# A DFT along time split by output index modulo 6, with score masks moved between engines and a new written order

## The chip, the core and the metric

The kernel runs on one core of a Trainium2 chip. The core has five engines that run side by side, each with its own queue in order: TensorE (PE in the profile, with weight loads as PEld) multiplies matrices into PSUM, VectorE (DVE), ScalarE (ACT) and GpSimd (POOL) do elementwise work, and SyncE (SP) here only starts DMA transfers. GpSimd does not read PSUM in this kernel; VectorE and ScalarE do. The metric is the device time of one execution in microseconds (us); lower is better.

## The reference: what is computed

Inputs are q, k, v of shape (4 batches, 8 heads, 768 steps, 64) and two weight matrices, 512 x 2048 and 2048 x 512. All are float32, and so is the output (4, 768, 512).

```
state = gamma[h] * state + outer(k[t], v[t]);  y[t] = (q[t] @ state) / 8      # for each batch and head, 768 steps
x     = y with the heads side by side: (4, 768, 512)
u     = x + real(fft over the 512 columns of (fft over the 768 steps of x))
un    = (u - mean(u)) / sqrt(var(u) + 1e-6)                                    # over the 512 columns
out   = u + relu(un @ w_ch1) @ w_ch2
```

gamma is 1 - 2^(-5-h) for head h, one constant a head.

## The kernel before

**Retention.** Steps are cut into 6 chunks of 128, heads into 4 pairs. Within a chunk the scores K Q^T are formed on TensorE, masked (causal, with a power of gamma folded in) and multiplied with V; between chunks a 64 x 64 state per head is carried. For batches 1 to 3 and pair i the units are: `lq`, `lk`, `lv` (or `l`) start the loads (L242); `cq`, `ck`, `cv` cast to float16 on GpSimd (L461 or L466, L477, L486); `t` or `tq`, `tk` transpose q and k, on TensorE with ScalarE copies (L655, L660, L665) or by DMA (L651, L673, L678); `s` builds the chunk states (L708, then L713 and L715); `a` makes and masks the scores of two chunks (`a_unit`: matmuls L689, one VectorE multiply with a table, L691; three units a pair); `y` forms the output of a head (L729, L732) and ScalarE writes it into x (L739).

**Mixing.** The DFT along time uses symmetries. `fs` (L758) adds and subtracts the two halves of the time axis, which separates even and odd output frequencies; `fd` (L785) and `fe` (L799, L801) do the like for the columns, giving `ee`: four groups (cosine or sine, two column blocks), each with a part for even and one for odd frequencies, each three blocks of 128 steps. A unit `f` (`s1_unit`) multiplies one group with a cosine or sine table (`csp`, `ssp`, 193 frequencies for each parity): two parities x three blocks, six matmuls of 193 columns (L861), and one copy that interleaves the parities into `g` (L864). `gr` makes a reversed copy (L868). `x` (`s2_unit`, L1015 to L1025) does the DFT along the columns and writes the rows of u, `X` adds x on GpSimd (L1048, L1050). `n` takes mean and variance on VectorE, `u` centres the row and rounds it to float16 on ScalarE (L1064), `r` is the root on ScalarE and the reciprocal on VectorE (L1074, L1076). Batch 0 has a layout of its own and is not touched.

**MLP.** `U` transposes the centred rows (by TensorE, L1087, or by DMA, L1083). Batch 0 runs as `i`, `h` and `c` with `O` (L1118, L1105, L1140, L1130). Batches 1 to 3 run as `H` (first matrix, L1193, with a relu, L1098 on ScalarE or L1095 on VectorE) and, for the second matrix, a scheme with seven products instead of eight: `w` and `j` form sums (L1181, L1211), `p` multiplies (L1242), `q` adds the product into the rows (L1256) and starts the output.

**Order.** Up to about 36 us a list FIRST is worked off (batch 0's retention and mixing, building of the tables). Then a written list LATER names every unit in the order in which it is issued. Each instruction is tied to the one before it on its own engine, so every engine's queue follows the list, and an instruction that waits holds back all that stand behind it on its engine. A name is the unit, its indices (batch, pair or row block, part) and, after @, the engine that evicts: a is ScalarE, v VectorE, s two halves on ScalarE, b one half on each, d a transpose by DMA. PSUM has five buffers for mixed use (`ps_g`) and, in this part, three for the MLP (`ps_pm`). SyncE's queue follows the list too: loads, DMA transposes and outputs.

Of the kernel before, what the change touches and what calls it, by code (L numbers as in the profile page):

```python
# [11 lines left out]
AF = mybir.ActivationFunctionType  # L12
ALU = mybir.AluOpType
f32 = mybir.dt.float32
# [5 lines left out]
P = 128  # L20
# [7 lines left out]
KN = 2 * NK  # L28
XW = 260
# [23 lines left out]
i02 U01@v Z x04 x03 i12 U02@a x05 i13 X04 i10 cq10 c0000 c0001 X05 TB l10 i20 l11 X03 l12 i22  # L53
cq11 l13 c0002 i11 i03 i21 n05 u05 ck10 n04 lq20 cv10 c0010 t10 w10 n03 u03 r00 c0003 i23 c0011
c0012 a101 s100 pz11 U03@a ck11 t11 c0020 a102 s101 a100 c0021 cv11 a110 s110 s111 ck12 u04 a112
cq12 c0013 y100 a111 cq13 c0022 cv12 U05@a ck13 cv13 y101 t12 U04@v c0023 O00 y110 O01 pz00 s120
h018@a s121 h012@a s130 y111 t13 h01C@v pz01 s131 lk20 a120 lv20 lq21 h017@a a122 pz10 h01A@a
h011@a a121 h013@v O02 h01D@a a131 a132 y121 y120 a130 h01B@a cq20 tq20 h015@a fs10 y131 y130
h01E@v h010@a h016@a fs11 fd10 g10 h014@a fd11 w20 fe11 c0100 ck20 tk20 h019@a lk21 lv21 lq22
lk22 fe10 w31 c0101 a201 c0102 r01 cv20 f110@a a202 f111@a f100@a f101@a g112 cq21 gr12@a a200  # L60
s200 cq22 h01F@a x11 tq21 X11 gr10@a c0110 x10 gr11@a lv22 s201 c0120 n11 X10 gr13@a n10 lq23
lk23 ck21 tk21 w11 c0121 c0122 w40 x12 u11 lv23 X12 cq23 u10 c0103 O03 c0111 c0112 cv21 U11@a
ck22 U10@v x14 n12 c0113 O04 c0123 y200 x13 H102@a a212 r10 x15 s210 X13 cv23 n13 y201 tq22
H107@a O05 H100@a a211 w21 a210 H106@a ck23 s211 u13 tk23 U13@d w30 H103@a H101@s j10104 w41
j10204 j10304 cv22 H105@a s230 u12 H104@s j10148 y210 tk22 y211 tq23 p101 q101 j10248 p102
j10404 q102 lq30 lk30 j10448 p104 p106 q106 lv30 lq31 j10348 U12@v p105 cq30 s231 p107 q105 s220
a221 a220 H112@a p103 q103 a231 a230 a232 X14 a222 s221 H110@a X15 n15 q107 ck30 H114@a n14
H115@s y231 lk31 y230 fs21 lv31 y220 lq32 y221 H113@s H116@s H111@s H117@s fs20 fd21 g20 u14
fd20 j11104 fe20 u15 j11148 U14@d r11 j11204 fe21 p111 q111 p112 cv30 j11404 j11248 p114 f200@a
p115 q115 f201@a tq30 j11448 gr21@a j11304 cq32 f210@a gr22@a U15@d f211@a p116 q116 gr23@a  # L70
j11348 g212 p113 cq31 lk32 gr20@a lv32 q112 q113 x20 X20 x21 p117 H124@a q117 tq31 x23 H120@s
H121@v H122@s ck31 X21 n21 x25 H123@a u21 n20 j12104 j12204 j12404 cv31 H125@a lq33 j12304
H127@a r12 tk31 H126@s j12148 x22 p121 p122 u20 q121 p124 p125 U21@d r20 j12248 p126 U20@d q122
q125 j12448 q126 X22 j12348 s300 s301 X23 tk30 p123 q123 n23 cq33 lk33 a312 p127 s310 H200@a
a301 u23 ck32 lv33 n22 H204@s q127 tk32 a300 H206@s a302 H203@a a311 u22 X25 x24 cv32 n25 H201@s
H202@a j20104 y300 a310 U23@d H205@s s311 U22@d H207@s j20148 y301 ck33 j20304 j20204 p201 q201
j20348 j20248 j20404 p204 p205 y310 X24 y311 q205 tq32 tk33 p206 q206 cv33 s330 p202 q202 s320
j20448 tq33 p207 n24 q207 H217@s u25 p203 a320 s321 q203 a331 u24 U24@d s331 H214@b a332 a330
# [20 lines left out]
def kernel(  # L99
# [241 lines left out]
    def qt_zeros():  # L341
        for j in range(2):
            nc.vector.memset(qts[j][0:D, 1], 0.0)
            nc.vector.memset(qts[j][D:P, 0], 0.0)

    m2 = const.tile([P, 1], f32, tag="m2c")
    odd = const.tile([P, 1], f32, tag="oddc")

# [1084 lines left out]
```

## Time and profile before

| | |
|---|---|
| three runs | 238.18, 238.02, 237.14 us, median 238.02 |
| profiled execution | 237.16 us, of which span 235.2 us |
| PE busy | 221.0 us, 94% of the span |
| DVE busy | 203.7 us, 87% |
| ACT busy | 137.5 us, 58% |
| POOL busy | 82.5 us, 35% |
| HBM | 27.26 MB read, 6.29 MB written |

How to read it: the span runs from the first to the last instruction of the profiled execution. Busy time of PE counts matmuls that overlap each other once; the length shown for a single matmul includes its way through the array, so the pace of a row of matmuls is read from the start of one group to the start of the next. In a row of the groups stand line, engine, operation, what is written and read with shapes and count, then busy us and mean ns of one, then the idle time ahead of them and what ended it. In a row of the timeline stand start, length, engine, line, operation and count, and in brackets the idle time before. TensorE has no idle time over 1.1 us after the first 36 us.

### The profile page before, as it was taken

The page shows a single profiled execution, that of the slowest core. Times are in us where ns is not written, and L with a number is a line of the kernel's source. Part 1 is how long each engine was busy: PE and PEld are TensorE (multiplying, and loading weights), DVE is VectorE, ACT ScalarE, POOL GpSimd, SP SyncE. Part 2 cuts the span into 40 slices and gives each one's busy share as a digit, 9 for nine tenths or more (in the row PEclk, how much of TensorE's full clock was granted, in tenths as well). Part 3 has the DMA queues.
Part 4 walks back from the last instruction along what each step waited for, and adds up shares of the span by engine and source line. Part 5 has one row for each costly group of instructions (what it writes and reads, how often), then busy time and mean ns, then how long its engine had stood idle before and what let it go on. Part 6 is the DMA issues. An engine that isn't in the chain of part 4 may idle for free.

```text
span 235.2 us, 6193 instructions
## 1 busy us (share of the span) xinstructions
PE 221.0 (94%) x2407; PEld 181.9 (77%) x2407; DVE 203.7 (87%) x505; ACT 137.5 (58%) x322; POOL 82.5 (35%) x148
## 2 busy tenths in 40 slices
PE   0888999998999999999999999999999999999993
PEld 0366778855776756999999999998999888898882
DVE  8799986887899999999999899989997996749673
ACT  5989758368777565751867735736529736062230
POOL 8378902654613076702604565500002330020000
PEclk9999999999999999999999999999999999999999
DMA  7999999999999999979699995894002140502202
GB/s 173 236 267 246 237 207 207 217 240 251 202 230 185 215 190 226 223 153 211 167 213 189 204 170 146 174 154 133 4 4 89 30 108 0 104 33 47 89 0 92
DMA packets 100956, 36.83 MB, mean 157 GB/s; under 512 B 91456, under 2 KB 97984, under 8 KB 100928
## 3 DMA queue, kind: packets, MB, share of 16 engines
q1 hardware_dynamic: 96704, 32.25, 68.3%
q0 software_dynamic: 4224, 4.19, 10.8%
q8 instruction: 19, 0.31, 0.6%
q14 instruction: 9, 0.07, 0.1%
HBM read 27.26 MB, written 6.29 MB: 143 GB/s over the span
## 4 chain that ended last, share of the span: by engine, by line
PE 65%; DMA 17%; DVE 4%; POOL 4%; SPq 3%; ACT 3%; issue 2%; POOLq 0%; ACTq 0%; DVEq 0%
PE psh L1193 27%; PE ps L1242 21%; DMA q<-in_q_dram 6%; DMA v<-in_v_dram 5%; PE psc L1140 3%; DMA wide<-in_k_dram 2%; PE wkA L689 2%; DMA k<-in_k_dram 2%; PE pq L1015 2%; PE ps L861 2%; DMA unT<-un 2%; PE ps L842 2%; SPq L242 1%; PE wkY L732 1%; PE pq L927 1%
## 5 line engine op out<-in xcount | busy, mean ns | idle before, releaser
L1098 ACT ACTIVATE ht<-psh 128x256 f16<-128x256 f32 (+2 forms) x112 | 49.3, 467 | 45.6 <-PE psh L1193 37.9
L1193 PE MATMUL psh<-unT,w 128*128 128x256 f16 x576 | 68.0, 273 | 0.2 <-DMA unT<-un 0.2
L1193 PEld LDWEIGHTS <-w 128*128 128x128 f16 x576 | 55.4, 98 | 6.8 <-DMA unT<-un 0.5
L1242 PEld LDWEIGHTS <-ht 128*128 128x128 f16 x440 | 41.3, 98 | 5.1 <-ACT ht L1098 0.5
L1048 POOL TENSOR_TENSOR u<-u,x 128x256 f32<-128x256 f32 x21 | 13.6, 646 | 68.4 <-DVE u L1022 57.3
L1242 PE MATMUL ps<-wide,ht 128*128 128x256 f16 x216 | 27.8, 273 | 0.0
L1211 DVE TENSOR_TENSOR ht<-ht 128x512 f16<-128x512 f16 (+2 forms) x57 | 22.4, 411 | 3.6 <-ACT ht L1098 3.4
L1140 PE MATMUL psc<-w,ht 128*128 128x512 f16 x96 | 23.5, 379 | 1.0 <-DVE ht L1095 1.0
L691 DVE TENSOR_TENSOR atm<-wkA,maskp 128x512 f16<-128x512 f32 x36 | 23.3, 677 | 0.0
L466 POOL TENSOR_SCALAR q16z<-q 128x384 f16<-128x384 f32 x16 | 8.4, 545 | 34.6 <-DMA q<-in_q_dram 23.3
L1095 DVE TENSOR_SCALAR ht<-psh 128x256 f16<-128x256 f32 (+2 forms) x25 | 13.5, 540 | 7.0 <-ACT ht L1098 5.5
L1242 PE MATMUL ps<-w,ht 128*128 128x256 f16 x144 | 18.3, 273 | 0.0
L715 DVE SCALAR_TENSOR_TENSOR s<-s,gk,wkK 128x128 f16<-128x128 f16 x48 | 16.3, 342 | 1.8 <-ACT s L713 0.5
L1064 ACT ACTIVATE un<-u,stats 128x512 f16<-128x512 f32 x21 | 14.7, 722 | 4.6 <-DVE stats L1060 4.6
L739 ACT ACTIVATE x<-wkY,gexp 128x384 f16<-128x384 f32 x24 | 13.1, 593 | 6.5 <-PE wkY L732 6.5
L477 POOL TENSOR_SCALAR kd<-k,gexp 128x384 f16<-128x384 f32 x22 | 12.7, 589 | 12.0 <-DMA k<-in_k_dram 11.0
L1256 DVE SCALAR_TENSOR_TENSOR u<-ps,stats,u 128x256 f32<-128x256 f32 (+2 forms) x27 | 15.2, 563 | 1.3 <-PE ps L1242 1.1
L1256 DVE SCALAR_TENSOR_TENSOR ob<-ps,stats,u 128x256 f32<-128x256 f32 (+2 forms) x27 | 14.8, 558 | 1.4 <-PE ps L1242 1.2
L1140 PEld LDWEIGHTS <-ht 128*128 128x128 f16 x96 | 9.0, 98 | 8.8 <-issue 1.1
L1059 DVE BATCH_NORM_STATS2 bst<-u 128x6 f32<-128x512 f32 x21 | 14.3, 681 | 0.7 <-POOL u L1050 0.7
L1050 POOL TENSOR_TENSOR u<-u,x 128x256 f32<-128x256 f32 x21 | 13.4, 636 | 0.0
L689 PE MATMUL wkA<-qTz,kT 128*128 128x256 f16 x72 | 12.5, 272 | 0.2 <-DVE atm L691 0.2
(203 smaller groups left out, 424.2 us busy)
## 6 DMA issues: line engine op xcount, KB each, us to landing
out_dram<-ob SPq DMA_DIRECT2D x23, 256.0 KB, 2.3
k<-in_k_dram SPq DMA_DIRECT2D x14, 384.0 KB, 5.4
v<-in_v_dram SPq DMA_DIRECT2D x14, 384.0 KB, 5.9
q<-in_q_dram SPq DMA_DIRECT2D x12, 384.0 KB, 6.5
w<-in_moe_w_ch_dram POOLq DMA_DIRECT2D x8, 512.0 KB, 10.8
wide<-in_q_dram SPq DMA_DIRECT2D x4, 384.0 KB, 5.9
wide<-in_v_dram SPq DMA_DIRECT2D x2, 384.0 KB, 6.0
wide<-in_k_dram SPq DMA_DIRECT2D x2, 384.0 KB, 5.7
```

The source lines that it names most:

```text
L689: nc.tensor.matmul(wk[:, c2], st["kT"][:, c, :], st["qT"][:, :, c, :], start=True, stop=True)
L691: nc.vector.tensor_tensor(out=st["atm"][:, 2 * part:2 * part + 2], in0=wk, in1=maskp[:, PAIR_ORDER[i]].unsqueeze(1).to_broadcast([P, 2, 2, ...
L715: nc.vector.scalar_tensor_tensor(out=s16[:, c], in0=s16[:, c - 1], scalar=gk2[:, hp:hp + 1], in1=wk[:, c - c0], op0=ALU.mult, op1=ALU.add)
L1048: nc.gpsimd.tensor_tensor(out=u[:, kb, 0:256], in0=u[:, kb, 0:256], in1=x[:, kb, 0, 1:257], op=ALU.add)
L1059: nc.vector.bn_stats(bst, u[:, kb, :])
L1064: nc.scalar.activation(un, u[:, kb, :], AF.Identity, bias=stats[:, kb, 0:1], scale=-1.0)
L1098: nc.scalar.activation(dst, src, AF.Relu, bias=0.0, scale=-1.0)
L1140: nc.tensor.matmul(psc_of[b, rb], ht16[:, fb, rb3 * P:(rb3 + 1) * P], w216[:, fb, :], start=(fb == 0), stop=(fb == NFB - 1))
L1193: nc.tensor.matmul(psh[:, t], w116[:, cb, fb * P:(fb + 1) * P], unT[:, cb, g * 256:(g + 1) * 256], start=(cb == 0), stop=(cb == 3))
L1211: nc.vector.tensor_tensor(out=out_, in0=x, in1=y, op=op)
L1242: nc.tensor.matmul(dst, lhsT, rhs[:, c0:c1], start=(n == 0 and (name is not None or k == 5 and m == 1)), stop=(n == 7), skip_group_check=True)
L1256: nc.vector.scalar_tensor_tensor(out=out_, in0=in_, scalar=r, in1=u_, op0=ALU.mult, op1=ALU.add)
```

## The change

Five things change together.

1. Units `z1`, `z2`, `z3` (`six_fold`) are new: five VectorE operations for each of batches 1 to 3 combine the three blocks of `ee` by sums and differences, into a new tile `zz` and in place. `s1_unit` then makes the output frequencies in six classes modulo 6, 64 or 65 columns each: four matmuls of 128 columns and two of 64 and 65 in place of six of 193. Its copy reads the six classes from PSUM at a stride of -64 and writes `g` in order. `zz` uses the buffer of `eo`.
2. Units `V00` to `V11` (`six_unit`) are new: ScalarE copies rearrange the tables `csp` and `ssp` in place, once, after batch 0 is done with them.
3. `a_unit` can mask by ScalarE and GpSimd: two ScalarE copies with a constant scale, one for each head, then a GpSimd `affine_select` in place that puts zeros below the diagonal. 25 of the 36 score units take it, 11 stay on VectorE.
4. `K0` (`root_unit`) runs a square root early on ScalarE, so that its table is loaded there. `u` may run on GpSimd (three of 21 do), and `x` gets a variant on ScalarE and GpSimd that the list does not use.
5. The list LATER is new. It holds the same units and the nine new ones. Some evictions go to another engine, and nearly all units move: the zero fills (`Z`) and the half tables (`TB`) come later, casts, loads, scores and folds of batches 1 to 3 mostly earlier.

```diff
+    def six_unit(e, part):
+        tab = tabs[e]
+        def run():
+            for par in range(2):
+                src = tab[:, par, 2 - 2 * part, 0:192].rearrange("p (m i) -> p i m", i=3)[:, ::-1]
+                if part == 0:
+                    src = src[:, 0:3:2] if par else src[:, 0:2]
+                n = 3 if part else 2
+                nc.scalar.copy(tab[:, par, 1 + part, 0:64 * n].rearrange(
+                    "p (s m) -> p s m", s=n), src)
+            if part:
+                nc.scalar.copy(tab[:, 0, 2, 192:193], tab[:, 0, 0, 192:193])
...
-    def a_unit(b, i, part):
+    def a_unit(b, i, part, eng):
...
+            dst = st["atm"][:, 2 * part:2 * part + 2]
+            if eng == "v":
+                nc.vector.tensor_tensor(
+                    out=dst, in0=wk,
+                    in1=maskp[:, PAIR_ORDER[i]].unsqueeze(1).to_broadcast([P, 2, 2, P]),
+                    op=ALU.mult)
+                return
+            for h2 in range(2):
+                nc.scalar.activation(dst[:, :, h2], wk[:, :, h2], AF.Copy, bias=0.0,
+                                     scale=float(gam[2 * PAIR_ORDER[i] + h2] ** (-P)))
+            nc.gpsimd.affine_select(out=dst, in_=dst, compare_op=ALU.is_ge, fill=0.0, base=0,
+                                    pattern=[[0, 2], [0, 2], [1, P]], channel_multiplier=-1)
...
+    def six_fold(b):
+        def run():
+            z = fd[b]["zz"] = fp.tile([P, 4, 6, P], f16, tag="eo", name="zz")
+            ee = fd[b]["ee"]
+            x0, x1, x2 = (ee[:, :, :, n] for n in range(3))
+            nc.vector.tensor_tensor(out=z[:, :, 0:2], in0=x1, in1=x2, op=ALU.add)
+            nc.vector.tensor_tensor(out=z[:, :, 2:4], in0=x2, in1=x1, op=ALU.subtract)
+            for par, op in ((0, ALU.subtract), (1, ALU.add)):
+                nc.vector.tensor_tensor(out=x1[:, :, par], in0=x0[:, :, par], in1=x1[:, :, par],
+                                        op=op)
+            nc.vector.tensor_tensor(out=x2, in0=x0, in1=z[:, :, 0:4:3], op=ALU.add)
...
     def s1_unit(b, e, cb, eng):
         def run():
-            tab = csp if e == 0 else ssp
-            ps = ps_g.tile([P, 2, NK], f32, tag="g", name="ps1", padded_shape=[P, 2, 256])
-            for par in range(2):
-                for sb in range(3):
-                    nc.tensor.matmul(ps[:, par, :], fd[b]["ee"][:, 2 * e + cb, par, sb, :],
-                                     tab[:, par, sb, :], start=(sb == 0), stop=(sb == 2))
-            dst = fd[b]["g"][:, 2 * e + cb].rearrange("p (i t) -> p t i", t=2)
-            (nc.vector.tensor_copy if eng == "v" else nc.scalar.copy)(dst, ps)
+            ps = ps_g.tile([P, KG], f32, tag="g", name="ps1", padded_shape=[P, 512])
+            t = ps[:, 0:384].rearrange("p (s m) -> p s m", s=6)
+            n = 2 * e + cb
+            ee, z, tab = fd[b]["ee"][:, n], fd[b]["zz"][:, n], tabs[e]
+            od, ev = (tab[:, par, 2, 0:192].rearrange("p (s m) -> p s m", s=3) for par in (1, 0))
+            for dst, x, w, y, v in (
+                    (t[:, 0:5:4], ee[:, 1, 1], od[:, 0:3:2], z[:, 1], tab[:, 1, 1, 0:128]),
+                    (t[:, 1:4:2], ee[:, 0, 1], ev[:, 0:2], z[:, 2], tab[:, 0, 1, 0:128])):
+                nc.tensor.matmul(dst, x, w, start=True, stop=False, skip_group_check=True)
+                nc.tensor.matmul(dst, y, v.rearrange("p (s m) -> p s m", s=2), start=False,
+                                 stop=True, skip_group_check=True)
+            nc.tensor.matmul(t[:, 2], ee[:, 1, 2], od[:, 1], start=True, stop=True,
+                             skip_group_check=True)
+            nc.tensor.matmul(ps[:, 320:385], ee[:, 0, 2], tab[:, 0, 2, 128:193], start=True,
+                             stop=True, skip_group_check=True)
+            src = bass.AP(tensor=ps.tensor, offset=ps[:, 320:321].offset,
+                          ap=[list(ps.ap[0]), [1, 65], [-64, 6]])
+            dst = fd[b]["g"][:, n].rearrange("p (m r) -> p m r", r=6)
+            (nc.vector.tensor_copy if eng == "v" else nc.scalar.copy)(dst, src)
...
+    def root_unit():
+        nc.scalar.activation(last[:, 4:5], epsT, AF.Sqrt, bias=0.0, scale=1.0)
```

Stretches of the new list that the prediction speaks of; the first is the start, then the first masks of batch 1 with `r00`, the load ahead of `a131`, the first new fold, and the last one:

```
i02 U01@v x04 X04 x03 i10 U02@a x05 i13 X05 i12 K0 cq10 Z c0000 c0001 i22 i20 i03 i11 ...
... t10 c0020 s100 c0021 cv11 s101 t11 r00 a100@a c0010 a102@v a101@v l13 cq12 s110 ck12 c0011 u05@a a111@v u03@a c0022 a110@a y100 ...
... y101 t12 lq20 s111 TB ... s130 h01C@a h012@a s131 a132@v cq20 a131@a y121 h015@a lv20 lq21 lk21 a130@v y120 ...
... y131 y130 lv21 cv21 O02 cv20 h017@a h010@a h014@a h01F@a h01E@a h011@a h013@a h019@a ck21 V11 fs10 h01D@a fs11 h01A@a fd10 fd11 g10 fe10 fe11 z1 h01B@v c0100 pz10 V01 a201@v c0110 f110@a f100@a ...
... fe31 u24@a U24@d p212 p216 p214 p215 q212 q216 p217 z3 j21404 j21448 g312 H220@a f301@v ...
```

In the list before, `r00` stands behind `t10 w10 n03 u03` and ahead of `c0003 i23 c0011 c0012`, and no root comes earlier; the `f` units follow `fe` of the same half.

More of the change, by code (lines that the diff above doesn't have):

```diff
@@ L59 @@
[L59 to L64, printed above, removed]
```

129 lines of the change are left out of this document (74 added, 55 removed).

## The prediction

> **What bounds the kernel now.** I read the page's engine sums first, then a table by stage, and TensorE's order of work at the places that the change touches. The page and the stage table (columns: length, busy us and instructions of PE, PEld, DVE, ACT, POOL, then TensorE clock, DMA share, GB/s):
>
> ```profile
> span 235.2 us, 6193 instructions
> PE 221.0 (94%) x2407; PEld 181.9 (77%) x2407; DVE 203.7 (87%) x505; ACT 137.5 (58%) x322; POOL 82.5 (35%) x148
> ...
> 50.00:80.00 30.00, 28.98 (x296) 19.67 (x295) 26.11 (x60) 22.00 (x41) 11.75 (x19) 1.00 1.14 222
> 80.00:120.00 40.00, 39.82 (x431) 32.67 (x429) 38.77 (x94) 24.60 (x64) 17.97 (x30) 1.00 1.09 200
> 120.00:170.00 50.00, 50.00 (x549) 45.40 (x548) 47.54 (x119) 29.33 (x75) 16.84 (x27) 1.00 0.77 151
> 170.00:200.00 30.00, 30.00 (x306) 27.09 (x304) 26.19 (x68) 16.91 (x42) 6.06 (x10) 1.00 0.17 45
> 200.00:231.00 31.00, 30.71 (x296) 26.97 (x294) 22.18 (x58) 9.38 (x26) 1.23 (x2) 1.00 0.23 56
> ```
>
> From 50 us on TensorE works 28.98 of 30, 39.82 of 40, then 50 of 50, 30 of 30 and 30.71 of 31 us, at full clock. So it sets the time, and a shorter stream of matmuls shortens the kernel, as long as it stays fed in its written order. VectorE is close behind (47.54 of 50), ScalarE is half idle. TensorE's idle time in these rows is 1.02 + 0.18 + 0.29 = 1.5 us, and 1.0 of that is one wait, shown below. The other views are TensorE's order of work (start, length, what, idle before and what ended it) and the groups of instructions of each engine (busy sum, mean ns, idle before).
>
> **The split by six (gain).** One unit of the old time-axis DFT is six matmuls of 193 columns; 12 such units run (batches 1 to 3). Their pitch is read from the starts of successive rows, not from the modelled lengths:
>
> ```profile
> 76.74 0.81 PE L1105 MATMUL psh<-unT,w 128*128 128x384 f16 x4
> 77.39 1.03 PE L1140 MATMUL psc<-w,ht 128*128 128x512 f16 x4
> 78.26 0.38 PE L689 MATMUL wkA<-qTz,kT 128*128 128x256 f16 x2
> 78.47 1.03 PE L1140 MATMUL psc<-w,ht 128*128 128x512 f16 x4
> 79.34 0.68 PE L861 MATMUL ps<-ssp,ee 128*128 128x193 f16 x6
> 79.85 0.38 PE L689 MATMUL wkA<-qTz,kT 128*128 128x256 f16 x2
> ...
> 72.64 0.31 PE L729 MATMUL wkY<-s,qTz 128*128 128x64 f16 x5
> 72.78 0.34 PE L732 MATMUL wkY<-v,atm 128*128 128x64 f16 x6
> 72.96 0.31 PE L729 MATMUL wkY<-s,qTz 128*128 128x64 f16 x5
> ...
> 128.38 0.40 PE L1015 MATMUL pq<-gk,g16r 128*128 128x129 f16 x4
> 128.61 0.27 PE L1193 MATMUL psh<-unT,w 128*128 128x256 f16 x1
> ```
>
> Six of 193 columns take 79.85 - 79.34 = 0.51 us. Four of about 128 take 128.61 - 128.38 = 0.23, eleven of 64 take 72.96 - 72.64 = 0.32, or 0.029 each. The new unit has four of 128 and two of 64 or 65: 0.23 + 0.06 = 0.29 us. Gain 12 x (0.51 - 0.29) = 2.6 us, all on the bounding engine. The page "TensorE: Matmul & The Clock Gate" of the Trainium skill, section "Back-to-back issue gap", speaks against this: it gives about 81 ns a matmul at 128 columns when each has its own weight load. By it the new unit would take 6 x 0.081 = 0.49 us and the gain would be 0.3 us. The rows above do not agree: with a weight load before each matmul, they show 57 ns at 128 columns and 29 ns at 64.
>
> **The fold for it (cost on VectorE).** `six_fold` adds five tensor_tensor in float16 for each batch: three on 1024 elements, two on 512. The same kind:
>
> ```profile
> L1181 DVE TENSOR_TENSOR wide<-w 128x1024 f16<-128x1024 f16 x2 | 1.4, 689 | 0.0
> L1211 DVE TENSOR_TENSOR ht<-ht 128x512 f16<-128x512 f16 x48 | 19.6, 427 | 2.1 <-ACT ht L1098 1.9
> L785 DVE TENSOR_TENSOR eo<-xab 128x768 f16<-128x768 f16 x12 | 6.1, 551 | 0.0
> L799 DVE TENSOR_TENSOR ee<-eo 128x768 f16<-128x768 f16 x6 | 3.4, 560 | 0.0
> L758 DVE TENSOR_TENSOR xab<-x 128x768 f16<-128x768 f16 x6 | 3.3, 589 | 0.0
> ```
>
> 3 x 0.69 + 2 x 0.43 = 2.9 us a batch, and the first `f` matmul waits for it. In batch 1 the new list puts 11 `h` units (0.65 us each: 77.39 - 76.74), two `c` parts (0.87 each: 79.34 - 78.47) and a score unit (0.21) between the last `y` and `f110`: 9.1 us of TensorE. VectorE's chain there is four `fs` (2.4), four `fd` (2.2), four `fe` (2.2), the mean row (0.5) and `z1` (2.9), 10.2 by means; queued instructions overlap by some 8% (L785: 12 x 551 ns in 6.1 us), and half of the `fs` can start before the last `y`. So TensorE waits 0 to 1.5 us; I take 0.6. In batch 2, 3.5 us of matmuls lie between `z2` and `f211`, in batch 3 under 1.1 but VectorE reaches `z3` early, behind two adds: 0 to 1, I take 0.3. `six_unit` rearranges the tables with nine ScalarE copies and one single-column one, about 2.5 us once, priced by the nearest rows; they are part of the ScalarE sum below. The eviction reads PSUM at a stride, 390 values for 386: the same 0.60 us, bounds 0 and +0.1 on ScalarE.
>
> ```profile
> L868 ACT COPY g16r<-g 128x384 f16<-128x384 f16 x11 | 5.4, 515 | 0.1
> L1017 ACT COPY qn<-pq 128x128 f32<-128x128 f32 x18 | 5.0, 279 | 5.2 <-PE pq L1015 4.8 <-DVE u L1025 0.3
> L864 ACT CAST g<-ps 128x386 f16<-128x386 f32 x12 | 6.7, 600 | 3.8 <-PE ps L861 3.6
> ```
>
> **The masks (VectorE to ScalarE and GpSimd).** 25 of 36 score masks leave VectorE: 5 in batch 1, 10 each in batches 2 and 3. Rows:
>
> ```profile
> L691 DVE TENSOR_TENSOR atm<-wkA,maskp 128x512 f16<-128x512 f32 x36 | 23.3, 677 | 0.0
> L1098 ACT ACTIVATE ht<-psh 128x256 f16<-128x256 f32 x62 | 21.1, 385 | 25.5 <-PE psh L1193 23.9 <-issue 1.5
> L299 POOL TENSOR_SCALAR_AFFINE_SELECT maskf<-maskf 128x128 f32<-128x128 f32 x1 | 0.3, 293 | 0.0
> L284 POOL MEMSET ht<- 128x512 f16 x1 | 0.5, 515 | 0.0
> masks.py:197 POOL MEMSET ident<- 128x128 f16 x1 | 0.2, 195 | 0.0
> ```
>
> VectorE loses 25 x 0.68 = 17 us and gets 8.7 back from the folds. ScalarE gets 25 x 2 x 0.385 = 19 us. A 512-element select is not in the trace: at the memsets' slope it is 293 + (515 - 195) = 0.61 us, at four times the 128 row 1.17; I take 0.61, since the 128 row holds a start-up too. GpSimd gets 15 us (up to 29) of which it has idle plenty. The mask's path grows from 0.68 to 0.77 + 0.61 and a hand-over, some 1.5 us. In the new list the last score unit of a pair stands 1.2 to 5.7 us of matmuls ahead of its first `y`, adding the pitches of the units between (before: 1.5 to 10.3), and in the tight pairs that last one is a VectorE mask. A select is queued behind casts that wait for loads, though (idle before, and what ended it):
>
> ```profile
> 63.84 0.99 POOL L466 TENSOR_SCALAR q16z<-q 128x384 f16<-128x384 f32 x2 [1.12 <-DMA q<-in_q_dram]
> 69.58 1.15 POOL L477 TENSOR_SCALAR kd<-k,gexp 128x384 f16<-128x384 f32 x2 [4.74 <-DMA k<-in_k_dram]
> 137.68 0.82 DVE L1211 TENSOR_TENSOR ht<-ht 128x512 f16<-128x512 f16 x1
> 139.56 1.50 POOL L466 TENSOR_SCALAR q16z<-q 128x384 f16<-128x384 f32 x2
> ```
>
> In the new list `cq20` stands right ahead of the select of `a131`, and its load is issued behind the key transposes of pair 2. I price that at 0 to 2 us, taking 0.4. The last two rows show a second cost: a VectorE add of two SBUF tensors at 0.82 for 0.43 while GpSimd adds, and a GpSimd cast pair at 1.50 for 0.99 while VectorE adds. The page "SBUF — State Buffer" of the Trainium skill, section "Who interferes with whom", has the rule: the two engines share one pair of ports, as a lock. The trace agrees. With 28 more GpSimd operations it happens more often; if a third of them hit, 9 x 0.4 = 4 us on VectorE, which has 8 more to spare.
>
> **Does ScalarE become the bound?** In 50 to 80 us it has 22.0 us. Five masks add 3.9, the tables 2.5, two relus taken from VectorE 1.0, and the table load leaves (1.3): 28.1 of 30. In 80 to 120 it has 24.6 + 7.7 = 32 of 40, in 120 to 170 29.3 + 7.7 = 37 of 50. Only the first is tight, and there two or three copies of transposes a pair go through ScalarE in order:
>
> ```profile
> L660 ACT COPY qTz<-tq 64x768 f16<-64x768 f16 x8 | 6.3, 789 | 0.1
> ```
>
> **The square-root table.** The 1.0 us wait of TensorE is this chain:
>
> ```profile
> 52.81 1.28 ACT L1074 ACT_TABLE_LOAD   x1
> 54.44 0.18 DVE L1076 RECIPROCAL stats<-stats 128x3 f32<-128x3 f32 x1 [2.05 <-ACT stats L1074]
> 54.53 0.66 DVE L1095 TENSOR_SCALAR ht<-psh 128x512 f16<-128x512 f32 x1
> 55.24 1.02 PE L1140 MATMUL psc<-w,ht 128*128 128x512 f16 x4 [1.02 <-DVE ht L1095]
> ```
>
> VectorE's reciprocal waits 2.05 us for the load and the root, and the relu that TensorE wants is queued behind it. In the new list the load is ahead of `c0000`, under 1.7 us of `c` matmuls that need no new relu, and the last relu stands ahead of `r00`. I take the whole 1.0 as gain; late next is the first masked `y`, behind the ScalarE copies of two pairs' transposes: 0 to 0.7, I take 0.2. The other edits (three casts to GpSimd, some relus between engines, the three zero fills later) sit on engines with idle time: nothing, bounds -0.3 and +0.5.
>
> **Sum** for the profiled execution of 237.16 us (span 235.2): -2.6 - 1.0 + 0.6 + 0.3 + 0.4 + 0.2 = -2.1, so 235.1. The three times shown run from 237.14 to 238.18 with median 238.02, so the profiled one is a low one; the median of the new kernel I put in between, 235.3.
>
> **Rivals.** Half a percent, 1.2 us, is about what a measurement of this kernel can tell from no change.
> A: ScalarE decides between 50 and 80 us. For: 28.1 of 30, and in-order copies of transposes (0.8 each) ahead of relus. Against: VectorE ran 38.77 of 40 in the next stage with TensorE at 39.82. Price: two late chains of two transposes' copies (0.8 to 1.5 us each) give back 1.6 to 3 us, time 236.9 to 238.3.
> B, the other side: selects come late on GpSimd. Place: pairs of batches 1 to 3 where a cast or residual add is ahead of a select. Decides when the select costs 1.17 us, or a load lands over 2 us after the mask's ScalarE half. Each late pair stops TensorE by 0.6 to 1.5 us; six of twelve pairs late is 3.6 to 9 us on top of the 235.3: 239 to 244. For: the 4.74 us wait above. Against: from 120 us on GpSimd was idle two thirds of the time.
> C: the split saves nothing, since a matmul's weight load bounds it: the unit stays at 0.5 us, time 235.3 + 2.3 to 2.6, 237.6 to 237.9. Against: the rows at 64 columns. The page on TensorE named above is its only support.
>
> **How the numbers follow.** Forecast (faster) 0.60, A 0.17, C 0.03, B 0.20. The likeliest one's own range is 233.3 to 236.8: the lower end takes every new wait as zero and the other edits at their -0.3 (237.16 - 3.9). The whole range reaches into B, to 240.0, leaving out half of B and a little below. Faster 0.60, same 0.20, slower 0.20.
>
> **What would show it.** Right: the new `ps1` matmuls at a pitch of 0.29 us a unit, the 1.0 us wait gone, TensorE's busy sum down by 2 to 3, masks' ScalarE halves at 0.39, selects near 0.6. Wrong: TensorE waiting on `atm` from GpSimd (B), on ScalarE copies or relus between 50 and 80 us (A), on `ee` or `zz` for more than 1.5 us, or 0.08 us a matmul (C).

## The result and the profile after

Twenty executions of each kernel gave a median of 237.03 us for the changed kernel (235.89 to 237.84) and 238.19 us for the kernel before (236.97 to 240.03). The ratio is 0.9955, 95% interval 0.9936 to 0.9975: 0.45% faster, and the medians differ by 1.2 us, where 2.9 (238.19 less 235.3) were forecast. The gain is clear of zero, but under the half percent that the prediction counted as no change. The profiled execution of the changed kernel took 237.41 us, 0.4 above its median, while the one before took 237.16, 1.0 below its median. So the two traces differ by +0.25 us where the medians differ by -1.2, and single waits have to be compared over several traces.

The page of the changed kernel (span, then busy us, share and instructions of each engine, then two of its costliest groups), and below it the stage table with the columns of the table before:

```profile
span 235.7 us, 6275 instructions
PE 220.4 (94%) x2407; PEld 179.0 (76%) x2407; DVE 197.5 (84%) x491; ACT 150.5 (64%) x383; POOL 102.6 (44%) x176
...
L724 POOL TENSOR_SCALAR_AFFINE_SELECT atm<-atm 128x512 f16<-128x512 f16 x25 | 15.9, 650 | 18.7 <-issue 11.7
L722 ACT ACTIVATE atm<-wkA 128x256 f16<-128x256 f32 x50 | 15.8, 395 | 5.3 <-PE wkA L712 5.1
```

```profile
50.00:80.00 30.00, 29.13 (x296) 19.40 (x296) 25.58 (x66) 25.81 (x63) 13.98 (x22) 1.00 1.08 227
80.00:120.00 40.00, 39.25 (x417) 31.22 (x415) 37.51 (x93) 29.00 (x84) 27.89 (x43) 1.00 1.18 218
120.00:170.00 50.00, 49.43 (x556) 44.30 (x555) 46.39 (x116) 34.06 (x94) 24.15 (x38) 1.00 0.70 133
170.00:200.00 30.00, 29.58 (x300) 26.39 (x300) 25.65 (x63) 15.96 (x44) 8.35 (x13) 1.00 0.21 49
...
```

The work did move as described: VectorE lost 6 us, ScalarE gained 13, GpSimd 20. But TensorE, which was without idle time from 120 to 200 us before, now shows 0.57 and 0.42 us of it there, and 0.75 instead of 0.18 in the stage from 80 to 120 us. Its busy sum fell by only 0.6 us, where the prediction named 2 to 3 as a sign of being right. TensorE's order of work shows the new units at their place (start, length, what), and its waits by place say what the new idle time is (what waited, what ended it, sum, times, longest):

```profile
78.92 0.22 PE L910 MATMUL ps<-ssp,ee 128*128 128x128 f16 x1
...
79.22 0.22 PE L910 MATMUL ps<-csp,ee 128*128 128x128 f16 x1
...
79.50 0.22 PE L910 MATMUL ps<-csp,ee 128*128 128x128 f16 x1
...
79.79 0.22 PE L910 MATMUL ps<-ssp,ee 128*128 128x128 f16 x1
...
80.08 0.38 PE L1206 MATMUL psc<-w,ht 128*128 128x512 f16 x1
```

```profile
PE psh L1259 <- DMA unT<-un: 1.1, 2, 0.7
PE wkK L739 <- POOL v L508: 1.0, 2, 0.6
...
```

Four units take 80.08 - 78.92 = 1.16 us, 0.29 each.

**A measure that sees small gaps.** The shown length of a matmul (220 ns at 128 columns) is longer than its pitch (56 ns), so a gap of up to some 0.16 us does not appear as idle time at all, and larger ones appear that much too short. For the comparisons below each trace was therefore divided in another way: from 36.3 us on, every matmul is given the median distance from its start to the next start for its number of columns (29 ns at 64, 56 at 128, 86 at 193, 109 at 256, 162 at 384, 216 at 512). The sum over all matmuls is the "pace"; what the real distances have beyond it is the "wait" (time lost to a lower clock counts into it, too). A record of one or two matmuls is missing in some traces, which moves the pace by 0.1 us.

| profiled execution | time, us | pace, us | wait, us |
|---|---|---|---|
| before | 237.16 | 190.81 | 3.73 |
| changed kernel | 237.41 | 188.00 | 7.01 |
| changed kernel, second trace | 237.15 | 188.11 | 6.65 |
| changed kernel, third trace | 236.21 | 188.0 | 5.45 |

The pace is 2.8 us shorter, as the split should make it. The wait is 1.7 to 3.3 us longer, and it eats most of the gain: between the first two rows -2.81 + 3.28 = +0.5, and the last matmul starts at 231.31 us instead of 230.86. The kernel before has only this one trace, of a low execution, so the new waits may look larger here than they are by the medians. The waits above 0.1 us, from the same distances, grouped by what ended them:

| us of wait | before | changed, three traces |
|---|---|---|
| relu behind the root (VectorE), 54 us | 1.18 | none |
| GpSimd casts of v and k, 49 to 53, 82 and 96 us | 0.44 | 2.07, 1.89, 1.12 |
| chunk states `s` (VectorE), 90 us | none | 0.54, 0.98, 0.47 |
| the fold (VectorE), 122 us | none | 0.26, 0.26, 0.25 |
| relu, and the row add `q`, 167 to 170 us | none | 0.81, 0.81, 0.81 |
| DMA transposes of rows, 190 and 204 us | 0.41 | 1.39, 0.70, 0.88 |

The rest of the waits above 0.1 us is alike, 1.0 us before and 1.0 to 1.1 in the changed kernel. The waits that an engine's order makes come back in all three traces (those for states differ by 0.5 us); those at loads and DMA transposes vary most.

Two of these places in the changed kernel's timeline (start, length, engine, line, operation, count, and in brackets the idle time before and what ended it):

```profile
49.69 0.83 POOL L508 TENSOR_SCALAR v<-v 128x768 f16<-128x768 f32 x1 [1.31 <-DMA v<-in_v_dram]
50.57 0.33 PE L739 MATMUL wkK<-v,kd 128*128 128x128 f16 x3 [0.59 <-POOL v L508]
...
80.31 2.51 POOL L508 TENSOR_SCALAR v<-v 128x768 f16<-128x768 f32 x2 [10.15 <-DMA v<-in_v_dram]
...
80.82 1.31 DVE L1247 TENSOR_TENSOR sd<-w 128x1024 f16<-128x1024 f16 x1
...
85.37 0.63 POOL L724 TENSOR_SCALAR_AFFINE_SELECT atm<-atm 128x512 f16<-128x512 f16 x1
...
86.56 0.63 POOL L1112 TENSOR_TENSOR u<-u,x 128x256 f32<-128x256 f32 x1
...
87.23 0.69 DVE L1121 BATCH_NORM_STATS2 bst<-u 128x6 f32<-128x512 f32 x1 [0.76 <-POOL u L1112]
...
90.39 0.98 DVE L746 SCALAR_TENSOR_TENSOR s<-s,gk,wkK 128x128 f16<-128x128 f16 x3
90.50 0.47 PE L760 MATMUL wkY<-s,qTz 128*128 128x64 f16 x4
91.17 0.19 PE L760 MATMUL wkY<-s,qTz 128*128 128x64 f16 x1 [0.19 <-DVE s L746]
```

In the first, the new list puts the state matmuls of batch 1's first pair ahead of the moment at which v is loaded and cast. In the second, GpSimd stands 10 us in front of a v that has not landed; then, from 80.31 us on, it works off casts, a select and residual adds in order without a break; VectorE waits 0.76 us for the second of those adds; and behind VectorE's queue the states of batch 2's first pair come 0.5 us late for TensorE. None of these waits needs a long operation. They come from what stands behind what, and beside what, in the new list: the casts run at the same time as VectorE's adds of weights (`sd`), and both are slow there, as the run without the split will show.

### The profile page after: what moved, and what is told of

It is laid out like the page before. It is cut to its first block, busy times and chain, and to the rows that moved or that the text cites. A ratio compares the mean times of both kernels' runs of the same rounds, so it can differ in the third digit from the quotient of the medians.

```text
span 235.7 us, 6275 instructions
## 1 busy us (share of the span) xinstructions
PE 220.4 (94%) x2407; PEld 179.0 (76%) x2407; DVE 197.5 (84%) x491; ACT 150.5 (64%) x383; POOL 102.6 (44%) x176
## 5 line engine op out<-in xcount | busy, mean ns | idle before, releaser
L1164 ACT ACTIVATE ht<-psh 128x256 f16<-128x256 f32 (+2 forms) x117 | 51.2, 467 | 38.9 <-PE psh L1259 37.0
L1259 PE MATMUL psh<-unT,w 128*128 128x256 f16 x576 | 66.8, 273 | 1.1 <-DMA unT<-un 1.1
L1277 DVE TENSOR_TENSOR ht<-ht 128x512 f16<-128x512 f16 (+2 forms) x57 | 23.8, 433 | 3.8 <-ACT ht L1164 3.3
L724 POOL TENSOR_SCALAR_AFFINE_SELECT atm<-atm 128x512 f16<-128x512 f16 x25 | 15.9, 650 | 18.7 <-issue 11.7
L499 POOL TENSOR_SCALAR kd<-k,gexp 128x384 f16<-128x384 f32 x22 | 14.1, 650 | 16.2 <-PE ps L915 12.4
L722 ACT ACTIVATE atm<-wkA 128x256 f16<-128x256 f32 x50 | 15.8, 395 | 5.3 <-PE wkA L712 5.1
L1161 DVE TENSOR_SCALAR ht<-psh 128x512 f16<-128x512 f32 (+2 forms) x19 | 10.7, 566 | 7.3 <-ACT ht L1164 3.5
L1130 ACT ACTIVATE un<-u,stats 128x512 f16<-128x512 f32 x18 | 13.0, 728 | 4.5 <-DVE stats L1122 4.5
L508 POOL TENSOR_SCALAR v<-v 128x768 f16<-128x768 f32 x11 | 10.1, 925 | 11.5 <-DMA v<-in_v_dram 11.5
```

The lines of the kernel that those rows point to most:

```text
L499: nc.gpsimd.tensor_scalar(out=kd[:, :, h2, :], in0=k32[:, h2], scalar1=gkd[:, h0 + h2:h0 + h2 + 1], scalar2=1.0, op0=ALU.mult, op1=ALU.mult)
L722: nc.scalar.activation(dst[:, :, h2], wk[:, :, h2], AF.Copy, bias=0.0, scale=float(gam[2 * PAIR_ORDER[i] + h2] ** (-P)))
L724: nc.gpsimd.affine_select(out=dst, in_=dst, compare_op=ALU.is_ge, fill=0.0, base=0, pattern=[[0, 2], [0, 2], [1, P]], channel_multiplier=-1)
L1130: nc.scalar.activation(un, u[:, kb, :], AF.Identity, bias=stats[:, kb, 0:1], scale=-1.0)
L1164: nc.scalar.activation(dst, src, AF.Relu, bias=0.0, scale=-1.0)
L1259: nc.tensor.matmul(psh[:, t], w116[:, cb, fb * P:(fb + 1) * P], unT[:, cb, g * 256:(g + 1) * 256], start=(cb == 0), stop=(cb == 3))
```

## The experiments

My theory after the result: the split's gain is real, but the new order spends it in waits. Rivals: the split gains less than the pace says because of its folds; the masks on GpSimd are what is late; the root's table load is worth nothing.

**The changed kernel again.** No edit; it measures how far a second trace and a second median differ.

> The changed kernel once more, unaltered: a second trace, to see which of TensorE's waits repeat, and its time beside the kernel before on one chip. Theory 'new order' (the split saves its 2.7 us of matmul pace in full, the root's wait is gone, and the new written order adds some 3 us of other waits): about 1.1 us (0.45%) faster than before, matmul pace after 36 us again 2.7 to 2.8 us shorter, waits over 0.1 us again near 6 us. If the waits are chance of one execution, they fall to about 3 us here and the time to 235.

Measured: 237.12 us, ratio 0.9954 (0.9932 to 0.9976). Pace and wait are in the table above. What follows: the result stands, and the waits at 90, 122 and 168 us are no chance.

**The split taken out of the new order.** The old units of six matmuls of 193 columns, no folds, no table copies, the rest of the new list as it is.

```diff
-                nc.tensor.matmul(dst, x, w, start=True, stop=False, skip_group_check=True)
...
+            for par in range(2):
+                for sb in range(3):
+                    nc.tensor.matmul(ps[:, par, :], fd[b]["ee"][:, 2 * e + cb, par, sb, :],
+                                     tab[:, par, sb, :], start=(sb == 0), stop=(sb == 2))
...
-fe10 fe11 z1 h01B@v c0100 pz10 V01 a201@v
+fe10 fe11 h01B@v c0100 pz10 a201@v
...
```

`V10`, `V00`, `V11`, `z2` and `z3` leave the list in the same way.

> The changed kernel without the split by six: old time-axis units of six matmuls with 193 columns, no z and V units, all else and the written order the same. 'New order': the split is worth its full 2.7 us, so this is 2 to 3 us slower than the changed kernel and 1 to 2 us slower than before. Rival 'folds' (the new VectorE folds and the wait for them eat the gain): within 1 us of the changed kernel.

Measured: 238.35 us, ratio to before 1.0023 (1.0002 to 1.0045), so 1.2 us more than the changed kernel in the same rounds. The pace is 190.92, the wait 4.76. The units are back at 193 columns, and the states at 90 us are there in time:

```profile
78.95 0.68 PE L904 MATMUL ps<-ssp,ee 128*128 128x193 f16 x6
...
79.57 0.68 DVE L1234 TENSOR_TENSOR sd<-w 128x1024 f16<-128x1024 f16 x1
...
80.39 1.63 POOL L506 TENSOR_SCALAR v<-v 128x768 f16<-128x768 f32 x2 [10.56 <-DMA v<-in_v_dram]
...
86.95 0.69 DVE L1108 BATCH_NORM_STATS2 bst<-u 128x6 f32<-128x512 f32 x1 [0.17 <-POOL u L1099]
...
90.81 0.31 PE L758 MATMUL wkY<-s,qTz 128*128 128x64 f16 x5
```

Slower than the changed kernel by 1.2 us lies between the two expectations, 2 to 3 and under 1. What follows: the split is worth 2.8 us of pace and costs 1.9 us of wait by the two traces of this chip (6.65 less 4.76), or 1.6 by the medians (2.8 less 1.2). Of the 1.9, only 0.26 is at the units that read the fold; another 0.98 appears ten microseconds later at the states; 0.57 is at the cast near 50 us, ahead of every unit of the split, and so is not its cost. The way to the states can be read here. Without the fold VectorE's first two adds of weights end (80.25 us) before GpSimd's casts begin. With it they fall on the casts: the second takes 1.31 us instead of 0.68, and the casts of v and of the keys behind them 4.13 to 4.15 us in the three traces instead of 3.29. The row statistics then start at 87.23 instead of 86.95, and the states 0.28 later as well (90.39 and 90.11), while TensorE, with its shorter units, is there 0.31 earlier (90.50 and 90.81). So a part of the gain turns into waiting for VectorE, which did not get faster. The new order without the split is no faster than the old one (238.35 beside 237.92), although the root's wait is gone from it and ScalarE and GpSimd take 25 masks off VectorE. The 0.81 us at 167 to 170 us and the waits at the casts are in its trace as well (0.53 + 0.28, and 0.61 + 0.46 + 0.24), so they are not the split's. Beside the waits of the kernel before without the root's (3.73 less 1.18 = 2.55), 2.2 us of new wait stand in this order even without the split.

**All masks back on VectorE, in the new order.**

All 25 score units with `@a` get `@v`, the first of them:

```diff
-r00 a100@a c0010 a102@v a101@v
+r00 a100@v c0010 a102@v a101@v
...
```

> The changed kernel with all 36 score masks on VectorE, order unchanged. Rival 'masks' (late selects on GpSimd and locked ports eat the gain): 1 to 2 us faster than the changed kernel. 'New order': the masks are not what TensorE waits for; 17 us more on VectorE, which then has 95% of some stages, make it 0 to 3 us slower than the changed kernel.

Measured: 248.57 us, ratio 1.0429 (1.0382 to 1.0475), 11.5 us more than the changed kernel. The pace is 188.0 and the wait 18.07 us. VectorE's busy sum is 211.4 us, and it is late in the tight places. The loss is far beyond the 0 to 3 us that were expected. The worst place (order of work, VectorE and then TensorE):

```profile
169.35 0.66 DVE L1119 BATCH_NORM_STATS2 bst<-u 128x6 f32<-128x512 f32 x1
...
170.15 0.66 DVE L714 TENSOR_TENSOR atm<-wkA,maskp 128x512 f16<-128x512 f32 x1
...
170.86 0.23 PE L761 MATMUL wkY<-v,atm 128*128 128x64 f16 x2 [1.90 <-DVE atm L714]
...
171.25 4.01 PE L1257 MATMUL psh<-unT,w 128*128 128x256 f16 x20
```

The mask stands behind row statistics on VectorE, and TensorE stands for 1.90 us. The last row shows something else: 20 matmuls of 256 columns take (4.01 - 0.27) / 19 = 0.197 us each, on average, where 0.109 is usual; the last section returns to it. What follows: in the new order the moved masks are needed; the order counts on VectorE being free of them.

**The early root taken out of the new order.**

```diff
-i13 X05 i12 K0 cq10 Z c0000
+i13 X05 i12 cq10 Z c0000
```

> The changed kernel without the early square root; the table load then falls in front of the first root of the list. If the early load is worth the 1.0 us wait that it was seen to cost before: 0.5 to 1.3 us slower than the changed kernel, with the wait back ahead of a c or y matmul near 55 us. If the new order hides the load anyway: within 0.3 us.

Measured: 237.78 us, ratio 0.9996 (0.997 to 1.0022), 0.66 us more than the changed kernel. Its profiled execution was its longest, 239.59 us, with a wait of 1.25 us that ends at 42.4 us, for a load of MLP weights; no other trace has one of that length there. Without the early unit the table load falls between the transposes' copies and the first ScalarE masks (ScalarE's order of work):

```profile
55.88 0.80 ACT L685 COPY kT<-tq 128x768 f16<-128x768 f16 x1
56.70 1.28 ACT L1138 ACT_TABLE_LOAD   x1
...
58.20 0.64 ACT L720 ACTIVATE atm<-wkA 128x256 f16<-128x256 f32 x2
```

TensorE then waits, up to 58.9, 59.6 and 60.4 us, for masks and states, 0.28 + 0.33 + 0.29 = 0.9 us in sum. What follows: the early load is worth 0.7 us by the medians (the intervals of the two kernels overlap) and 0.9 by the waits.

**Each part alone, in the old order.** These three ask whether a part carries its gain without the new list. First the early root:

```diff
-i12
+i12 K0
```

> The kernel before with the early square root alone, in the old order: 0.5 to 1.2 us faster than before, the 1.0 us wait near 55 us gone. If the load then delays the first relus instead: within 0.3 us.

Measured: 237.32 us, before 238.10 on the same chip, ratio 0.9975 (0.9951 to 1.0). Pace 190.81, wait 3.34. ScalarE and TensorE at the new place of the load:

```profile
39.86 1.28 ACT L1418 ACT_TABLE_LOAD   x1
...
41.99 0.61 ACT L1149 ACTIVATE ht<-psh 128x512 f16<-128x512 f32 x1
...
42.65 0.55 PE L1169 MATMUL psh<-unT,w 128*128 128x128 f16 x7 [0.59 <-ACT ht L1149]
```

The old wait of 1.18 us is gone, but the load delays a relu, and 0.75 + 0.12 us of wait stand there instead: by the waits the gain is 0.4, by the medians 0.8. In the old order it gains a half of what was forecast for it, or somewhat more.

Then the masks: the same 25 units as in the new list get `@a`, the first two of them:

```diff
-a100
+a100@a
...
-a110
+a110@a
...
```

> The kernel before with the same 25 masks on ScalarE and GpSimd, in the old order, nothing else. TensorE did not wait for masks there, but for VectorE's queue at one place (1.0 us behind the root): within 0.8 us of before. If VectorE's 17 us are what the old order lacked: 1 to 2 us faster. If late selects stop TensorE in an order not made for them: 2 us slower or more.

Measured: 245.09 us, ratio 1.03 (1.0259 to 1.0341); pace 190.92, wait 11.23. GpSimd's and TensorE's order of work at one of the late pairs:

```profile
115.18 3.00 POOL L721 TENSOR_SCALAR_AFFINE_SELECT atm<-atm 128x512 f16<-128x512 f16 x5
118.14 0.63 POOL L1096 TENSOR_TENSOR u<-u,x 128x256 f32<-128x256 f32 x1
118.73 0.64 POOL L1098 TENSOR_TENSOR u<-u,x 128x256 f32<-128x256 f32 x1
119.32 0.64 POOL L721 TENSOR_SCALAR_AFFINE_SELECT atm<-atm 128x512 f16<-128x512 f16 x1
...
120.01 0.23 PE L760 MATMUL wkY<-v,atm 128*128 128x64 f16 x2 [0.97 <-POOL atm L721]
...
120.40 3.79 PE L1245 MATMUL psh<-unT,w 128*128 128x256 f16 x18
```

Five selects in a row hold GpSimd for 3.00 us, the sixth stands behind two residual adds, and TensorE waits 0.97 us for it. This is the mechanism of rival B, 1.1 us above rival B's range (239 to 244), but in the old order: the new list keeps it away. By the distances the selects cost 0.55 + 0.46 + 1.13 us here; the low clock behind them and other late units make up the rest of the 7.5 us of wait that this trace has more than the kernel before. Again the 256-column matmuls right behind run at about twice their pitch, (3.79 - 0.27) / 17 = 0.207 us.

Last the split:

```diff
-i22
+i22 V10 V00 V11 V01
...
-fe10
+fe10 z1
...
-fe21
+fe21 z2
...
-fe30
+fe30 z3
```

> The kernel before with the split by six alone, in the old order, masks all on VectorE: each fold right behind the second half of fe, the table copies in an idle stretch of ScalarE near 45 us. Matmul pace 2.8 us shorter; but VectorE has no room there: the folds (2.6 us a batch) go into waits for the f units, for masks and states. Expected 0 to 4 us slower than before; if the folds are hidden without the masks' move, 2 to 2.7 us faster.

Measured: 251.05 us, ratio 1.0561 (1.0509 to 1.0613). The pace is 187.89, the shortest of all, and the wait 22.53. TensorE's and VectorE's order of work at the first fold:

```profile
78.69 1.03 PE L1203 MATMUL psc<-w,ht 128*128 128x512 f16 x4
78.81 0.56 DVE L827 TENSOR_TENSOR ee<-eo 128x768 f16<-128x768 f16 x1
...
81.05 0.69 DVE L889 TENSOR_TENSOR zz<-ee 128x1024 f16<-128x1024 f16 x1
...
82.37 0.76 DVE L892 TENSOR_TENSOR ee<-ee 128x512 f16<-128x512 f16 x2
...
83.19 0.29 PE L907 MATMUL ps<-ssp,ee 128*128 128x128 f16 x1 [3.47 <-DVE ee L892]
83.28 0.31 PE L908 MATMUL ps<-ssp,zz 128*128 128x128 f16 x1
83.38 0.31 PE L907 MATMUL ps<-ssp,ee 128*128 128x128 f16 x1
```

The chain of `fe` and fold, 78.81 to 83.13 us, now stands in front of units that have only 0.9 us of `c` matmuls ahead of them. Each of the three batches pays 3.5 to 4.4 us for it, and behind each wait the pitch at 128 columns is 0.10 us for 0.056. What follows: the split and the masks have no gain of their own in the old order, and the root's 0.8 us lies at the edge of what can be told (interval up to 1.0). The larger distance that the new list puts between producer and reader makes the split and the masks possible; the waits listed above came with the same list.

**Mending the order.** If the waits are the order's, moving the units that wait should give time back. The changed kernel with its list altered at five places, which the diff shows in seven pieces:

```diff
-t10 c0020 s100 c0021 cv11 s101 t11 r00 a100@a c0010 a102@v
+t10 c0020 c0021 s100 cv11 s101 c0010 t11 r00 a100@a a102@v
...
-lv23 w31 s201
+lv23 s201
...
-y200 y201 c0113
+y200 y201 w31 c0113
...
-p112 f211@a j11448 g212
+p112 g212 f211@a j11448
...
-H212@s H215@s H216@a H217@a j21148 j21348 j21248 H211@a H213@a j21104 j21304 r21 j21204 p211
+H212@s H211@a H213@a H215@s j21104 j21304 j21204 H216@a H217@a j21148 j21348 j21248 r21 p211
...
-H224@s j22148 u31@a
+H224@s u30@a U30@d j22148 u31@a
...
-j22304 u30@g U30@d gr30@a
+j22304 gr30@a
```

Besides, `c0003` went ahead of `a110`, `U33@d` directly behind `u33`, and `u32@a U32@d` ahead of `p301`; `u30`, as the diff shows, also went from GpSimd to ScalarE.

> The changed kernel with only its written list altered at the five places where TensorE was seen to wait in both of its traces: chunk-state and transpose units of pairs 0 and 1 of batch 1 moved behind second-matrix parts of batch 0 (wait for a cast of v behind its load, 0.8 to 1.2 us, and for keys, 0.5), w31 moved behind the first y of batch 2 (wait for the state on VectorE, 0.5 to 1.0), g212 ahead of f211 (0.26), the H units of batch 2's second group in the order in which the products read them (0.8), and row centring and DMA transposes of batch 3's first two groups issued earlier (0.7 to 1.4). 'New order': these waits are the lost gain, so it is 2 to 3.5 us faster than the changed kernel, 233.5 to 235, 1.3 to 1.9% below before. If waits only move on to the next late thing: within 1 us of the changed kernel.

Measured: 236.63 us, before 238.10, ratio 0.9953 (0.9928 to 0.9978). Wait 5.96. The waits aimed at are gone, but others are in their places (waits of TensorE by place, columns as above):

```profile
PE ps L1306 <- DVE u L1320: 0.8, 1, 0.8
PE psh L1257 <- DVE unT L1152: 0.6, 1, 0.6
PE psh L1169 <- DVE ob L1194: 0.6, 1, 0.6
PE wkK L737 <- ACT qTz L680: 0.5, 1, 0.5
```

What follows: of 2 to 3.5 us of wait that were to go, about 0.7 to 1 went (5.96 beside 6.65 and 7.01), and none beside the changed kernel's third trace (5.45). The time is the same as the changed kernel's by the ratios, 0.9953 and 0.9955. A wait that is moved away shows the next one behind it. A second alteration went for those, and a third for what was left of them:

```diff
-cq12 s110 ck12 c0011
+cq12 c0011 s110 ck12
...
-y201 w31 c0113
+y201 c0113
...
-O04 a211@a
+O04 w31 a211@a
...
-p112 g212 f211@a j11448
+p112 j11448 g212 f211@a
...
-p212 p216 p214
+p212 p214 p216
```

> The mended list altered again at the four places to which its waits had moved: a c part in front of s110 (0.6 us behind a copy of q's transposes), w31 behind O04 (0.8 us for the last transposes of batch 2's... of batch 1's first row blocks), p214 ahead of p216 (0.9 us for an add on VectorE), j11448 ahead of g212 (0.6 us for a sum). If waits can be mended one at a time, 1.5 to 2.5 us faster than the mended kernel, near 234.5. If TensorE is now held by the sum of VectorE's and ScalarE's queues, waits move on again and it gains under 0.8 us.

Measured: 235.82 us, before 237.73, ratio 0.9913 (0.9886 to 0.994). Wait 4.91. That is 0.8 us less than the first alteration took on another chip (1.0 by the ratios), so it lies between the two expectations.

The third, on top of the second:

```diff
-X03
+X03 TB
...
-y101 t12 lq20 s111 TB
+y101 O00 t12 lq20 s111
...
-cv13 O00
+cv13
```

> mended2 with the half tables TB (2.6 us of VectorE) back near 45 us, where VectorE is idle a third of the time, and the first output row O00 two units earlier: the wait of 0.7 us for a buffer that O00 and O01 free near 63 us should go. 0.4 to 0.8 us faster than mended2; if the row adds are late for another reason, within 0.3 us.

Measured: 236.02 us, ratio 0.9919 (0.989 to 0.9948). The wait it was made for (0.73 us for the output row's add at 63 us) is gone, and three others of 0.60, 0.35 and 0.55 us came: wait 5.09, no gain over the second. (In the diff `O00` moves ahead by some 20 units, not by two.)

**The second alteration beside the changed kernel**, both on one chip.

> The changed kernel once more, on the same chip as the next run, so that the two can be compared directly. Theory (what the split and the root save goes in part into waits of TensorE that the new order brings): 0.9955 of the kernel before, waits of TensorE after 36 us again 6.6 to 7.1 us. Rival (the medians of different chips differ by chance, and the altered order is worth nothing): the same time as the next run within 0.2 us.

> The altered order with the fewest waits, beside the changed kernel on one chip. Theory: its waits of TensorE are some 4.9 us, 1.7 to 2.1 fewer, so it is 1 to 2 us faster than the changed kernel in the same rounds, ratio to the kernel before 0.989 to 0.993. Rival: no difference, ratio 0.995 to 0.996 as there.

Measured: the changed kernel 236.48 us, ratio 0.995 (0.9933 to 0.9966), wait 5.45; the altered one 235.70 us, ratio 0.9934 (0.99 to 0.9968), wait 5.08. Eight of the altered kernel's twelve times lie between 235.2 and 235.8 us, below the shortest of the changed kernel here (235.84), but the other four lie between 238.4 and 239.8, and none of these has a trace. What follows: the altered order is faster than the kernel before, by 0.7 to 0.9%. That it is faster than the changed kernel is likely (0.8 us by the medians, 0.4 by the ratios) but not settled, since the intervals overlap. Its wait is 0.4 us less in these two traces, where 1.7 to 2.1 were expected: the changed kernel's wait in this trace was 1.2 us less than in the trace of the earlier chip, at the loads and transposes above all, so the size of what can be mended varies with them.

## Why the prediction was wrong

The sign was right, but the gain was less than half of what was forecast, and the cause was none of the rivals. That 237.03 lies in the stated range is luck: it is above the likeliest case's own range (233.3 to 236.8) and inside the whole one only because that reached into rival B, which did not come.

1. **The split (forecast -2.6).** Right: 0.29 us a unit as forecast, 2.8 us of pace by the traces. TensorE's busy sum was the wrong sign to name for it: it fell by 0.6, since the shown lengths cover small gaps. Rival C is out. It is the floor that the rule from the Trainium skill (page "TensorE: Matmul & The Clock Gate", section "Back-to-back issue gap") would have made: a unit of six would take 0.49 us by it, and 0.29 is measured.
2. **The fold (forecast +0.9 of wait).** At the reading units 0.26 us in batch 2 and none above 0.1 in batches 1 and 3, less than forecast. But without the split the wait is 1.9 us less by the traces, 1.6 by the medians. The prediction looked only at the first reader of the fold, not at what VectorE had behind it: `z1` pushes VectorE's adds onto GpSimd's casts, and that, with TensorE's earlier arrival, gives late states at 90 us (0.5 to 1.0 us in the three traces, none without the split). It had seen that adds and casts slow each other and set 4 us of it against VectorE's spare time, so at nothing; spare time elsewhere did not help the reader here.
3. **The masks (forecast +0.4).** Prices right: 650 ns for the select (0.61 estimated, so the upper bound of 1.17 is out) and 395 ns for the ScalarE half (385). No `y` of batches 1 to 3 waits over 0.1 us for a select in the changed kernel's three traces, so rival B did not come, nor did the wait at `a131`. GpSimd's queue does show, though by another way: residual adds behind slow casts and a select hold VectorE's row statistics at 87 us (0.63 to 0.76 us). It takes the split as well: the same wait is 0.17 us without it, and 0.17 with all masks on VectorE.
4. **ScalarE as the bound (rival A).** It worked 25.8 of 30 us between 50 and 80 us, 28.1 were forecast, and no large wait there is ScalarE's. Out.
5. **The root (forecast -1.0, +0.2).** The 1.18 us wait is gone, as forecast. Its worth is 0.7 us in the new order and 0.4 to 0.8 in the old one; the load has to stand somewhere on ScalarE, and in the old order it delayed a relu by 0.75.
6. **The step that failed** is "The other edits ... nothing, bounds -0.3 and +0.5", together with the sum's 1.5 us for all new waits. The prediction priced the operations that the new list adds and treated the moving of nearly every unit as free, because the engines concerned had idle time. Beside the waits of before without the root's (3.73 - 1.18 = 2.55), the three traces have 4.5, 4.1 and 2.9 us of new wait for the forecast 1.5; by the medians it is 2.8 (-2.8 - 1.2 + 2.8 = -1.2). Most of it stands at edits that were not looked at one by one: states ahead of the load and cast of their v, sums and relus of `H` and `p` in another sequence, transposes by DMA closer to their readers. Idle time of an engine over a stage said nothing about them. With the measured terms the sum for the profiled execution is 237.16 - 2.81 + 3.28 = 237.6, where 237.41 was measured; the remaining 0.2 lies outside the span, which itself grew by 0.5 us (235.2 to 235.7).
7. **The base was a second wrong step.** The terms gave -2.1 for the profiled execution of 237.16, to 235.1, and the new median was put only 0.2 above that, although the same paragraph calls the profiled execution a low one. It lies 1.0 below its kernel's median of 238.19; -2.1 from there is 236.1. So of the 1.7 us between 235.3 and 237.03, 0.8 is this step, and 0.9 the terms: new waits 1.3 over, the split and the root 0.2 each better than forecast.

That waits of the new order took the gain is shown by the traces. How they divide is shown in part: 2.2 us stand there without the split, and the rest comes with it. The new order with all three parts taken out was not run, so order and masks are not told apart, and the kernel before has one trace only. Which single displacement made which wait was tried only in groups, by the altered lists, and there new waits came up; so the share of each displacement stays open.

## What to carry to other kernels

When a change comes with a new hand-written order, price the order: walk along the bounding engine in the new list and ask for each unit what its latest operand is, what stands ahead of that operand's producer on its own queue, and when its load is issued. Do this for the second and third reader behind an inserted block too. Judge the bounding engine by the distances between starts, not by its busy sum, and test a part both taken out of the new order and put into the old one, since here two of the three parts cost 7 and 13 us when put alone into the old order.

## What the runs showed of the hardware

- **The clock goes by the idle share of fixed stretches of 3.41 us.** In the traces' clock records TensorE's granted clock is 1.00 or 0.50 and changes only at multiples of 3.413 us from its first rise: a low stretch lasts 3.41 or 6.83 us. With all masks on VectorE, three such stretches in a row (the stage table's columns; the clock is the one after GpSimd's) show it:

```profile
168.03:171.44 3.41, 1.38 (x28) 1.11 (x26) 3.34 (x8) 1.17 (x3) 0.00 (x0) 1.00 0.20 77
171.44:174.85 3.41, 3.41 (x18) 2.45 (x17) 3.34 (x8) 2.15 (x6) 0.00 (x0) 0.50 0.23 82
174.85:178.27 3.42, 3.42 (x34) 3.03 (x32) 2.20 (x8) 2.38 (x6) 0.00 (x0) 1.00 0.19 38
```

In the first, waits of 0.30 and 2.06 us by the distances (1.90 of idle time shown) make 2.36 us; in the second, 256-column matmuls run at 213 ns for 109. Five times in the fourteen traces, from 14 us on, the clock fell while the program ran, each time behind a stretch with 2.0 us of wait or more: 2.36 here, 2.02 with the masks moved in the old order (0.55, 0.46 and most of 1.13), 2.63, 3.35 and 3.18 with the split in the old order. No stretch with 1.78 us or less brought a fall, though such stretches hold single waits of up to 1.5 us. So the bound lies between 1.8 and 2.0 us of 3.41 in these runs. One low stretch holds some 1.6 us of loss (15 matmuls at 0.104 us more), on top of the wait's own length. The changed kernel stays below the bound: at most 1.5 us in a stretch, and its pitch did not change. The Trainium skill, page "TensorE: Matmul & The Clock Gate", section "The HAM clock gate", tells of such a clock with two states, half and full, and gives about 3.4 us of idleness for the fall to half. The half rate agrees with 213 for 109 ns; the falls after 2.0 and 2.36 us of wait here came earlier than that.
- **One kernel's waits differ between executions by over 1.5 us** (7.01, 6.65, 5.45 in three traces), most at the places that depend on loads and DMA transposes. One trace of each kernel puts the change at +0.25 us where the medians say -1.2.
